# An attention-and-MLP kernel: a 224-byte gap ahead of x's transposed tiles, and the layernorm of tiles 6 and 7 moved behind two evacuations

## The chip, the core and the metric

The kernel runs on one core of a Trainium2 chip. The metric is the device time of one execution in microseconds; the number of record is the median of several runs. A core has five engines that run beside each other, each working through its own instructions in order: TensorE (PE in the profile, with its weight loads shown apart as PEld), VectorE (DVE), ScalarE (ACT), GpSimd (POOL) and SyncE (SP), which here only starts transfers. ScalarE starts some transfers too.

## The reference

Input x has 2048 rows of 512 numbers. The output is x + s * g, with

```python
xn = _layernorm(x)                        # over the 512 columns
q, k, v = xn @ wqkv                       # 32 heads of 16
# each row attends to 8 rows: itself and the rows 2, 4, ..., 14 before it
s = softmax(q . k / 4) @ v, then @ wo
h = relu(xn @ w1 + b1) ** 2               # 1792 wide
g = silu(h @ w2 + b2)
```

All in float32. A product of float32 accuracy is made here of three fast products: each operand is split in a high part and a low part (the rounding error of the high part), and high*high, high*low and low*high are summed (`PASSES`).

## The kernel before

Rows are worked on in 16 tiles of 128 rows. Phase 1 makes, tile by tile, the layernorm, the transpose and the three products q, k and v. Phase 2 runs over 4 chunks of 4 tiles and makes the MLP (`up` writes `ph`, `down` writes `pb`) and the output product (`pw`). VectorE does the sliding attention underneath, in units of 256 rows, from phase 1 on to the end of phase 2; `pump` places its steps in the program by a planner's clock (`clock["PE"]`, `clock["V"]`, priced from constants). Only operations of TensorE and VectorE advance that clock.

Order. Operations of TensorE, VectorE, ScalarE and GpSimd are kept in program order on their engine (`Ordered`). Transfers on SP are ordered by the framework's scheduler; those on ScalarE (the loads of q, k and v for attention) stand in ScalarE's order. Transfers share eight completion semaphores in turn.

Phase 1 in steps, for tile t:

- `load_x(t)` brings x; four buffers `x` in turn.
- `mean(t)` and `spread(t)` (tiles 6 to 15): ScalarE passes over x with a running sum (writing `scratch`), and GpSimd makes `rs` and `shift` of the sums. Tiles 0 to 5 use VectorE's statistics instead (`stats`).
- `norm(t)` writes `xn` (tiles 6 to 15: on ScalarE, from x, `shift` and `rs`) and starts the load of x for tile t + 4. From tile 4 on, two tiles share one buffer `xn`, and there is only one such buffer.
- `shuffle(t)`, t even: four transfers of 128 KB on SP copy `xn` to `xb` with partitions rearranged. The buffer `xn` is free for the next pair when these have landed.
- `trans(t)`: a transpose of `xb` on VectorE into PSUM (`pxT`), then on ScalarE the high part into `xt[t][:, 0]`. `lowx(t)`: VectorE writes the low part. Tiles 0 to 3 are transposed by TensorE and their parts lie in `xT` instead of `xt`.
- `qkv(t, s)`, s = 0, 1, 2 for q, k, v: 12 matrix products `pq` = 128x512, the part of x as weights (stationary), a part of `wq` streamed. Four PSUM buffers in turn. `evacuate(t, s)`: ScalarE copies `pq` to `stg`; after the odd tile of a pair SP stores the pair (`sq`, `sk`, `sv`).

The main loop of phase 1 (`for a in range(2, NT, 2)`, b = a + 1) issues for each pair the six calls `qkv(a,0)`, `qkv(b,0)`, `qkv(a,1)`, `qkv(b,1)`, `qkv(a,2)`, `qkv(b,2)`, and between them the layernorm of the pair a + 4, the transposes of the pair a + 2, and attention steps by `pump`. Ahead of the loop stand `qkv(0,2)`, `norm(4)`, `norm(5)`, `shuffle(4)`, `mean(6)`, `qkv(1,2)`, `spread(6)`, `mean(7)`.

Addresses. Pools of phase 1 are laid out one after the other: `px`, `pstg`, `pxT`. Inside a pool a tile name gets its slots in the order of first use, each slot rounded up to 32 bytes of a partition. From the start of `px` to the first `xt` there are x 4 x 2048 bytes, `st` 2 x 32, `mv` 2 x 32, `rs` 3 x 32, `xb` 2 x 4096, `scratch` 2048, `xn` 4096, `mean` 3 x 32, `shift` 3 x 32 and `stg` 4 x 4096. All weight buffers, the `xT` buffer and the `h` buffers ahead of `px` are multiples of 512 bytes long. Phase 2's pool takes the place of the three pools when they are closed.

Of the kernel before, what the change touches and what calls it, by code (L numbers as in the profile page):

```python
# [8 lines left out]
F32 = mybir.dt.float32  # L9
# [5 lines left out]
P = 128  # L15
# [37 lines left out]
def body(ctx: ExitStack, tc: tile.TileContext, x, wqkv, wo, w1, b1, w2, b2, out):  # L53
# [32 lines left out]
    PE, V, A, G = Ordered(nc.tensor, "PE"), Ordered(nc.vector, "V"), Ordered(nc.scalar), Ordered(nc.gpsimd)  # L86
# [15 lines left out]
    def psA(name):  # L102
        return psum.tile([P, 512], F32, name=name, tag="acc", bufs=4)
# [25 lines left out]

    p1ctx = ExitStack()  # L130
    px, pstg, pxT = (p1ctx.enter_context(tc.tile_pool(name=n, bufs=1)) for n in ("px", "pstg", "pxT"))
    xins = {}


# [4 lines left out]
    def load_x(t):  # L139
        xins[t] = px.tile([P, D], F32, name=f"x{t}", tag="x", bufs=4)  # L140
        dma(xins[t], tile_rows(x, t))
# [217 lines left out]
    def pump(margin=-SLACK):  # L359

        limit = clock["PE"] + margin
        flush(clock["PE"])
        while True:
            if coming[0] is None:
                coming[0] = next(stream, None)
            if coming[0] is None or clock["V"] + coming[0] > limit:
                break
            coming[0] = next(stream, None)
        if coming[0] is None:
            not_before(limit)  # L370
# [4 lines left out]
    def load_w(f):  # L375
        r1, r2 = (piece(f"{n}{f}") for n in ("w1r", "w2r"))
        dma(r1.rearrange("p (k c) -> p k c", c=P), w1[:, f * P:(f + 1) * P].rearrange("(k p) c -> p k c", p=P))
        dma(r2, w2[f * P:(f + 1) * P, :])
        raws[f] = r1, r2

    def next_w():

        f = len(w12)
        if f < NF:
            w12[f] = buffer(f"w{f}", HOME[f]) if f in HOME else p2.tile([P, 2, 2, 512], FR, name=f"w{f}")
            for i, r in enumerate(raws.pop(f)):
                split(w12[f][:, 0, i], w12[f][:, 1, i], r, G)
            if f + 2 < NF:
                load_w(f + 2)


    NT = S // P
# [9 lines left out]
    def small(name, t):  # L402
        return px.tile([P, 1], F32, name=f"{name}{t}", tag=name, bufs=3)

    def scratch(t):
        return px.tile([P, D], F32, name=f"scratch{t}", tag="scratch")
# [6 lines left out]
    def spread(t):  # L413
        rs[t], shifts[t] = small("rs", t), small("shift", t)
        A.activation(scratch(t), xins[t], AF.Square, bias=means[t], accum_out=rs[t])
        G.tensor_scalar(rs[t], rs[t], 1.0 / D, 1e-5, op0=OP.mult, op1=OP.add)
        G.tensor_tensor(rs[t], rs[t], mhalf, op=OP.pow)
        G.tensor_mul(shifts[t], means.pop(t), rs[t])
# [6 lines left out]
    def norm(t):  # L425

        src = xins.pop(t)
        if t < TURN:
            xn[t] = dst = px.tile([P, 2, D], F32, name=f"xn{t}", tag="xb", bufs=2)[:, 0]
        else:  # L430
            if t % 2 == 0:
                xn[t] = px.tile([P, 4, 2, P], F32, name=f"xn{t}", tag="xn")
            dst = xn[t // 2 * 2][:, :, t % 2].rearrange("p a (k c) -> p k a c", k=KT)
            src = src.rearrange("p (k a c) -> p k a c", a=4, k=KT)
        if t < STATS:
            halves = [slice(0, D // 2), slice(D // 2, D)] if t == 0 else [slice(None)]
            for i in halves:
                V.tensor_scalar(dst[:, i], src[:, i], mv[t][:, 0:1], rs[t], op0=OP.subtract, op1=OP.mult)
        else:
            A.activation(dst, src, AF.Identity, bias=shifts.pop(t), scale=rs[t])  # L440
        if t + 4 < NT:
            load_x(t + 4)
# [7 lines left out]
    def shuffle(t):  # L450

        src = xn.pop(t)
        xb[t] = px.tile([P, 4, 2, P], F32, name=f"xb{t}", tag="xb", bufs=2)
        for a in range(4):
            dma(xb[t][32 * a:32 * a + 32].rearrange("p b e c -> p b (e c)"), src[:, a].rearrange("p e c -> p (e c)"))  # L455

    def trans(t):
        place(t)
        pTs[t] = psT(f"pxT{t}")
        if t < TURN:  # L460
            for kt in range(KT):
                PE.transpose(pTs[t][:, kt * P:(kt + 1) * P], xn[t][:, kt * P:(kt + 1) * P], ident)
            seen[t] = clock["PE"] + 800
        else:

            V.transpose(out=pTs[t].rearrange("p (k n b) -> p b k n", k=KT, b=4),
                        in_=xb[t // 2 * 2][:, :, t % 2].rearrange("p b (k c) -> p b k c", k=KT))
            seen[t] = clock["V"] + 800
        A.activation(xt[t][:, 0], pTs[t].rearrange("p (k n) -> p k n", k=KT), AF.Copy)

    def lowx(t):
        not_before(seen.pop(t))
        V.tensor_sub(xt[t][:, 1], pTs.pop(t).rearrange("p (k n) -> p k n", k=KT), xt[t][:, 0].bitcast(F32))
# [3 lines left out]
    def qkv(t, s, between=None, late=False):  # L477

        ps = psA(f"pq{t}_{s}")
        order = [(kt, a, b) for kt in range(KT) for a, b in PASSES]  # L480
        if late:
            order.sort(key=lambda o: o[1])
        for n, (kt, a, b) in enumerate(order):
            PE.matmul(ps, xt[t][:, a, kt], wq[2 * s + kt // 2][:, b, kt % 2, :], start=n == 0, stop=n == 11)
            if between and n == 5:
                between()
        evacuate(t, s, ps)

    def evacuate(t, s, ps):
        if t % 2 == 0:  # L490
            stgs[s] = pstg.tile([P, 4, 2, P], F32, name=f"stg{t}_{s}", tag="stg", bufs=4)
        A.activation(stgs[s][:, :, t % 2], ps.rearrange("p (g c) -> p g c", g=4), AF.Copy,
                     scale=0.25 if s == 0 else 1.0)
        if t % 2:
            r0 = (t - 1) * P + (0 if s == 0 else HALO)
            dst = (sq, sk, sv)[s][:, r0:r0 + UP, :].rearrange("g (p e) c -> p g (e c)", e=2)
            dma(dst, stgs[s].rearrange("p g e c -> p g (e c)"))
            done = done_tiles["qkv"[s]]
            done[0] = t + 1
            done[1][t // 2] = clock["PE"]  # L500
# [8 lines left out]
    def up(c, f):  # L509
        ph = psH(f"ph{c}_{f}")  # L510
        n = 0
        for kt in range(KT):
            for a, b in PASSES:
                PE.matmul(ph.rearrange("p (j n) -> p j n", n=P), w12[f][:, a, 0, kt * P:(kt + 1) * P],
                          xT[c][:, :, b, kt, :], start=n == 0, stop=n == 11)
                n += 1
        if f == NF - 1 and c + 1 < NCH:
            load_xT(c + 1)
        h = hpool.tile([P, 2, 512], FR, name=f"h{c}_{f}", tag="h", bufs=3)
        A.activation(ph, ph, AF.Relu, bias=b1t[:, f:f + 1])  # L520
        A.activation(h[:, 0], ph, AF.Square)
        A.activation(ph, ph, AF.Square)
        hs[f] = h, ph, clock["PE"] + 2000

    def lowh(f):
        h, ph, t = hs[f]
        not_before(t)
        V.tensor_sub(h[:, 1], ph, h[:, 0].bitcast(F32))
# [69 lines left out]
    for a in range(2, NT, 2):  # L598
        b, more, later = a + 1, a + 2 < NT, a + 6 < NT
        if a >= TPC:  # L600
            for t in (a, b):
                dma(sx[t // TPC][:, t % TPC], xt[t].bitcast(F32))
        if a + 4 < NT:
            norm(a + 4)
            spread(b + 4)
        qkv(a, 0)
        pump(LATE)
        if a + 4 < NT:
            norm(b + 4)
            shuffle(a + 4)  # L610
        qkv(b, 0)
        if more:
            trans(a + 2)
        pump(LATE)
        qkv(a, 1)
        if more:
            lowx(a + 2)
            trans(b + 2)
        pump(LATE)
        if not more:  # L620
            up(0, 0)
        qkv(b, 1)
        if more:
            lowx(b + 2)
        if a == 2:
            load_w(0)
            load_w(1)
        else:
            next_w()
        if not more:  # L630
            pump()
            up(0, 1)
            lowh(0)
        pump(LATE)
        qkv(a, 2)
        if later:
            mean(a + 6)
        pump(LATE)
        qkv(b, 2)
        if later:  # L640
            spread(a + 6)
            mean(b + 6)
        if a == NT - 4:
            dma(b1t, b1.rearrange("(f p) -> p f", p=P))
        pump(LATE if more else -SLACK)
# [193 lines left out]
```

## Time and profile before

| what | value |
|---|---|
| median of 3 runs | 502.01 us (501.7 to 502.99) |
| span of the profiled execution, first to last instruction | 500.6 us |
| TensorE (PE) busy | 491.6 us, 98% of the span |
| VectorE (DVE) busy | 422.9 us, 84% |
| ScalarE (ACT) busy | 212.2 us, 42% |
| GpSimd (POOL) busy | 133.4 us, 27% |
| mean granted TensorE clock | 0.997 |

The time of the profiled execution itself is not among those listed; its span lies 1.4 us under the median, and what lies around a span (start and end of the program) is counted in the time alone. In the profile's rows a line such as `38.26 0.81 ACT ... [9.79 <-DMA xb<-xn]` reads: starts at 38.26 us, takes 0.81 us, and the engine sat idle for 9.79 us before it, until the transfer named had landed. Rows of TensorE give the start of a group, the time to the end of its last product, and the count; each product's end is pipelined into the next one's start.

### The profile page before, as it was taken

What the parts mean: (1) busy time and instruction counts of PE and PEld (TensorE: products, weight loads), DVE (VectorE), ACT (ScalarE), POOL (GpSimd) and SP (SyncE); (2) the same over time, 40 slices, a digit from 0 to 9 for tenths busy, and PEclk for the clock granted to TensorE, in tenths of its full rate; (3) what the DMA queues carried; (4) which work ended last, traced back from release to release, by engine and by line L of the source; (5) the groups of instructions that cost most, each with busy time, mean ns of one, the idle gap of its engine ahead of it and who ended that gap; (6) DMA issues with size and microseconds to landing.
All of it is one profiled execution on the core that took longest, in us unless ns stands there. A gap on an engine that the chain in (4) does not pass through costs nothing.

```text
span 500.6 us, 5874 instructions
## 1 busy us (share of the span) xinstructions
PE 491.6 (98%) x2154; PEld 402.8 (80%) x2154; DVE 422.9 (84%) x352; ACT 212.2 (42%) x377; POOL 133.4 (27%) x123
## 2 busy tenths in 40 slices
PE   8997999999999999999999999999999999999997
PEld 6876888888888888888888888888888888888886
DVE  5905599999889699997999998899999889996235
ACT  5526556652344465515424342441254256214331
POOL 1312255343427499200223002041300022220000
PEclk9998999999999999999999999999999999999999
DMA  8996989969966975644216416152333705121022
GB/s 292 283 287 187 324 293 332 289 200 331 310 234 236 206 252 140 201 168 158 101 26 241 156 44 259 67 216 68 117 126 97 269 2 199 43 84 64 22 84 85
DMA packets 48520, 88.79 MB, mean 177 GB/s; under 512 B 5372, under 2 KB 32364, under 8 KB 45676
## 3 DMA queue, kind: packets, MB, share of 16 engines
q1 hardware_dynamic: 44172, 54.87, 35.1%
q10 hardware_dynamic: 4320, 33.56, 18.8%
q8 instruction: 17, 0.28, 0.2%
q14 instruction: 11, 0.09, 0.0%
HBM read 57.94 MB, written 27.32 MB: 170 GB/s over the span
## 4 chain that ended last, share of the span: by engine, by line
PE 95%; DMA 3%; ACT 0%; DVE 0%; SPq 0%; issue 0%; POOL 0%; ACTq 0%; POOLq 0%
PE ph L82 30%; PE pb L82 30%; PE pq L82 25%; PE pw L82 9%; DMA xb<-xn 2%; DMA x<-in_A_x 1%; PE pxT L82 0%; SPq L455 0%; ACT scratch L82 0%; DVE z L82 0%; ACT xn L82 0%; DVE st L82 0%; POOL rs L82 0%; ACT stg L82 0%; DVE xn L82 0%
## 5 line engine op out<-in xcount | busy, mean ns | idle before, releaser
L82 PE MATMUL pb<-w,h 128*128 128x512 f32 x672 | 160.6, 389 | 0.0
L82 PEld LDWEIGHTS pb<-w,h 128*128 128x128 f32 x672 | 126.1, 188 | 26.2
L82 PE MATMUL ph<-xU,w 128*128 128x512 f32 x504 | 120.6, 389 | 0.0
L82 PEld LDWEIGHTS ph<-xU,w 128*128 128x128 f32 x504 | 94.6, 188 | 19.6
L82 ACT ACTIVATE ph<-ph,b1t 128x512 f32<-128x512 f32 x56 | 37.0, 660 | 159.6 <-PE ph L82 150.6
L82 PE MATMUL pq<-wq,xt 128*128 128x512 f32 x432 | 101.3, 395 | 0.0
L82 PEld LDWEIGHTS pq<-wq,xt 128*128 128x128 f32 x432 | 81.1, 188 | 19.7
L82 DVE TENSOR_TENSOR pr<-k,q 128x2048 f32<-128x2048 f32 x32 | 77.6, 2425 | 1.6 <-DMA q<-sq 1.2
L82 DVE TENSOR_TENSOR pv<-v,L 128x2048 f32<-128x2048 f32 x32 | 74.2, 2320 | 0.6
L82 DVE TENSOR_REDUCE L<-pr 128x128 f32<-128x2048 f32 x32 | 72.9, 2278 | 0.6
L82 DVE TENSOR_REDUCE v<-pv 128x256 f32<-128x2048 f32 x32 | 72.9, 2279 | 0.6
L82 DVE TENSOR_TENSOR h<-ph,h 128x512 fp32r<-128x512 f32 x56 | 38.0, 679 | 31.9 <-ACT ph L82 31.9
L82 PE MATMUL pw<-wot,oT 128*128 128x512 f32 (+1 forms) x204 | 45.9, 376 | 0.0
L82 POOL TENSOR_TENSOR z<-z,xr 128x512 f32<-128x512 f32 x12 | 25.5, 2127 | 67.1 <-DVE z L82 57.7
L82 PEld LDWEIGHTS pw<-wot,oT 128*128 128x128 f32 x204 | 36.8, 188 | 7.1
L82 ACT ACTIVATE stg<-pq 128x512 f32<-128x512 f32 x48 | 28.2, 593 | 31.4 <-PE pq L82 28.0
L82 POOL TENSOR_TENSOR w<-w1r,w 128x512 fp32r<-128x512 f32 x14 | 29.4, 2098 | 44.9 <-ACT w L82 40.0
L82 PE MATMUL ph<-xT,w 128*128 128x512 f32 x168 | 40.5, 390 | 0.0
L82 PEld LDWEIGHTS ph<-xT,w 128*128 128x128 f32 x168 | 31.5, 188 | 6.7
L82 PE MATMUL pq<-wq,xT 128*128 128x512 f32 x132 | 32.7, 408 | 3.6 <-ACT stg L82 3.6
L82 ACT ACTIVATE h<-ph 128x512 fp32r<-128x512 f32 x56 | 33.7, 602 | 1.8
L82 PEld LDWEIGHTS pq<-wq,xT 128*128 128x128 f32 x132 | 25.5, 196 | 10.3 <-ACT stg L82 4.1
(64 smaller groups left out, 330.4 us busy)
## 6 DMA issues: line engine op xcount, KB each, us to landing
k<-sk ACTq DMA_DIRECT2D x8, 1408.0 KB, 8.3
v<-sv ACTq DMA_DIRECT2D x8, 1408.0 KB, 6.5
sx<-xt SPq DMA_DIRECT2D x12, 512.0 KB, 6.2
xU<-sx ACTq DMA_DIRECT2D x6, 1024.0 KB, 8.6
x<-in_A_x SPq DMA_DIRECT2D x16, 256.0 KB, 4.5
sk<-stg SPq DMA_DIRECT2D x8, 512.0 KB, 4.5
sq<-stg SPq DMA_DIRECT2D x8, 512.0 KB, 5.8
q<-sq ACTq DMA_DIRECT2D x8, 512.0 KB, 9.0
```

What stands on the lines that cost most here:

```text
L82: return tc.keep_in_program_order(f(*a, **k))
```

## The change

First, a tile of 56 float32 numbers per partition (224 bytes) is made in the pool `pxT` ahead of all others, so the `xt` buffers lie 224 bytes further on; GpSimd clears it once. Second, in the pass a = 2 of the main loop the calls that make the layernorm of tiles 6 and 7 and its rearrangement no longer stand around `qkv(2,0)`, but behind `qkv(3,0)`; the order among them is changed as well.

```diff
     px, pstg, pxT = (p1ctx.enter_context(tc.tile_pool(name=n, bufs=1)) for n in ("px", "pstg", "pxT"))
+    G.memset(pxT.tile([P, 56], F32, name="gap"), 0.0)
     xins = {}
...
         if a >= TPC:
             for t in (a, b):
                 dma(sx[t // TPC][:, t % TPC], xt[t].bitcast(F32))
-        if a + 4 < NT:
+        if 2 < a and a + 4 < NT:
             norm(a + 4)
             spread(b + 4)
         qkv(a, 0)
         pump(LATE)
-        if a + 4 < NT:
+        if 2 < a and a + 4 < NT:
             norm(b + 4)
             shuffle(a + 4)
         qkv(b, 0)
+        if a == 2:
+            spread(7)
+            norm(6)
+            norm(7)
+            shuffle(6)
         if more:
             trans(a + 2)
         pump(LATE)
```

ScalarE's order in that pass was: `norm(6)`, `spread(7)`, evacuation of `qkv(2,0)`, `norm(7)`, evacuation of `qkv(3,0)`, high part of tile 4. It becomes: evacuation of `qkv(2,0)`, evacuation of `qkv(3,0)`, `spread(7)`, `norm(6)`, `norm(7)`, high part of tile 4.

## The prediction

> **What bounds the kernel now.** I read the page first, then TensorE's timeline, then who makes it wait.
>
> ```profile
> span 500.6 us, 5874 instructions
> ...
> PE 95%; DMA 3%; ACT 0%; DVE 0%; SPq 0%; issue 0%; POOL 0%; ACTq 0%; POOLq 0%
> ...
> L82 PE MATMUL pq<-wq,xt 128*128 128x512 f32 x432 | 101.3, 395 | 0.0
> ...
> L82 PE MATMUL pq<-wq,xT 128*128 128x512 f32 x132 | 32.7, 408 | 3.6 <-ACT stg L82 3.6
> ```
>
> The chain that ended last is TensorE for 95% of the span, so time is won only where TensorE idles or runs slower than it can. Two rows are odd: products with weights `xt` take 395 ns, and those with `xT` (tiles 0 to 3) contain an idle time of 3.6 us, ended by an evacuation on ScalarE. TensorE's timeline of the early part:
>
> ```profile
> 20.07 16.60 PE L82 MATMUL pq<-wq,xT 128*128 128x512 f32 x72
> 40.31 7.36 PE L82 MATMUL pq<-wq,xT 128*128 128x512 f32 x24 [3.65 <-ACT stg L82]
> 47.51 22.79 PE L82 MATMUL pq<-wq,xt 128*128 128x512 f32 x97
> ```
>
> and of the change of phases:
>
> ```profile
> 139.91 2.93 PE L82 MATMUL ph<-xT,w 128*128 128x512 f32 x12
> 142.68 2.96 PE L82 MATMUL pq<-wq,xt 128*128 128x512 f32 x12
> 145.48 2.93 PE L82 MATMUL ph<-xT,w 128*128 128x512 f32 x12
> ...
> 156.60 2.88 PE L82 MATMUL pb<-w,h 128*128 128x512 f32 x12
> 159.32 2.88 PE L82 MATMUL ph<-xT,w 128*128 128x512 f32 x12
> ```
>
> From start to start, twelve products take 2.72 us at 156.60 (226.7 ns each), but 2.80 at 142.68. Between 47.51 and 139.91 stand 33 groups, 396 products in 92.40 us: 233.3 ns each. The same by stages (columns: busy us and count of PE, PEld, DVE, ACT, POOL, then granted clock, DMA share, GB/s):
>
> ```profile
> 20.00:36.60 16.60, 16.60 (x75) 13.48 (x73) 4.40 (x11) 4.24 (x10) 2.72 (x7) 1.00 0.94 265
> 36.60:40.30 3.70, 0.07 (x1) 0.00 (x0) 0.73 (x1) 2.00 (x4) 0.36 (x2) 1.00 0.44 147
> ...
> 41.10:44.50 3.40, 3.40 (x9) 2.61 (x8) 1.33 (x2) 2.49 (x5) 0.00 (x0) 0.50 0.44 139
> ...
> 47.50:139.90 92.40, 92.40 (x397) 74.33 (x396) 84.12 (x64) 46.27 (x94) 38.55 (x44) 1.00 0.92 297
> 156.60:210.00 53.40, 53.40 (x237) 44.23 (x236) 47.92 (x33) 29.69 (x52) 38.87 (x22) 1.00 0.77 227
> ```
>
> After the idle time the granted clock is 0.50 for 3.4 us: the stall is paid twice. Why ScalarE is late, and what stands behind it:
>
> ```profile
> 26.43 0.58 ACT L82 ACTIVATE stg<-pq 128x512 f32<-128x512 f32 x1
> ...
> 38.26 0.81 ACT L82 ACTIVATE xn<-x,shift,rs 128x512 f32<-128x512 f32 x1 [9.79 <-DMA xb<-xn]
> 38.98 0.71 ACT L82 ACTIVATE scratch<-x,mean 128x512 f32<-128x512 f32 x1
> ...
> 39.68 0.57 ACT L82 ACTIVATE stg<-pq 128x512 f32<-128x512 f32 x1
> 41.01 0.81 ACT L82 ACTIVATE xn<-x,shift,rs 128x512 f32<-128x512 f32 x1 [0.75 <-POOL shift L82]
> 41.73 0.58 ACT L82 ACTIVATE stg<-pq 128x512 f32<-128x512 f32 x1
> 42.21 0.59 ACT L82 ACTIVATE xt<-pxT 128x512 fp32r<-128x512 f32 x1
> ...
> 44.19 0.60 ACT L82 ACTIVATE xt<-pxT 128x512 fp32r<-128x512 f32 x1 [0.91 <-DVE pxT L82]
> 44.20 0.54 ACTq L82 DMA_DIRECT2D v<-sv  x1
> ...
> 52.69 0.82 ACT L82 ACTIVATE xn<-x,shift,rs 128x512 f32<-128x512 f32 x1 [2.92 <-issue]
> ...
> 54.11 0.58 ACT L82 ACTIVATE stg<-pq 128x512 f32<-128x512 f32 x1
> 56.55 0.81 ACT L82 ACTIVATE xn<-x,shift,rs 128x512 f32<-128x512 f32 x1 [1.86 <-POOL shift L82]
> 57.27 0.58 ACT L82 ACTIVATE stg<-pq 128x512 f32<-128x512 f32 x1
> ```
>
> `norm(6)` (38.26) waits 9.79 us for the one buffer `xn`, until `shuffle(4)` has landed. Behind it stand the evacuations of `qkv(2,0)` (39.68) and `qkv(3,0)` (41.73), whose products (36 and 48 after 20.07) were done at 28.4 and 31.1. TensorE runs on through the four PSUM buffers and stops at `qkv(2,2)`, which needs the first one back.
>
> **The layernorm behind two evacuations.** The two evacuations then run at about 28.5 and 31.2, before ScalarE waits, so `qkv(2,2)` follows at once. The last product before the stall ends at 20.07 + 16.60 = 36.67; a product's end overlaps its successor by 2.88 - 2.72 = 0.16 us, so `qkv(2,2)` can start at 36.51 and `qkv(4,0)` 5.44 us later, at 41.95, instead of 47.51. That is 5.56 us: 3.80 of idle time and 1.76 of half clock.
>
> The wait of `norm(6)` stays; behind it now stand `norm(7)`, the high parts of tiles 4 and 5 and the evacuations of `qkv(2,1)` and `qkv(3,1)`. At ScalarE's own spacing (0.72 us from layernorm to the next instruction, 0.48 per copy) `norm(7)` starts at 38.98, tile 4's high part at 39.70, the evacuation of `qkv(2,1)` at 40.2, tile 5's high part at 41.7, that of `qkv(3,1)` at 42.3. `qkv(4,0)` (41.95) needs the third and `qkv(5,0)` (44.7) the last: they hold by 1.2 and 1.9 us. VectorE's transpose of tile 4 waits for the same landing as before. If that cover were gone, each us would be paid on TensorE.
>
> What is late next is the pair after it.
>
> ```profile
> 35.27 0.39 SPq L497 DMA_DIRECT2D sv<-stg  x1
> 39.10 3.08 SPq L141 DMA_DIRECT2D x<-in_A_x  x2
> 42.27 2.50 SPq L455 DMA_DIRECT2D xb<-xn  x4
> 44.87 0.78 SPq L497 DMA_DIRECT2D sq<-stg  x1
> ```
>
> ```profile
> xb<-xn SPq DMA_DIRECT2D x12, 128.0 KB, 5.4
> ```
>
> ```profile
> 52.64 0.73 DVE L82 STREAM_TRANSPOSE pxT<-xb 128x512 f32<-128x512 f32 x1 [2.60 <-DMA xb<-xn]
> ...
> 58.37 0.69 DVE L82 TENSOR_TENSOR xt<-pxT,xt 128x512 fp32r<-128x512 f32 x1 [2.83 <-ACT xt L82]
> ```
>
> The moved steps issue two loads of x and the four transfers of `shuffle(6)` on SP. These follow `norm(7)`, which starts 2.03 us earlier, so they go out at about 40.24 instead of 42.27. The store `sq` of tiles 2 and 3 (44.87) no longer waits for a late evacuation; I expect it ahead of the loads of x, right behind `sv` at 35.27. Its four pieces go out 0.63 us apart, the last at 42.1. `shuffle(6)` took until 52.6, 8.4 us after its last issue, where a piece lands in 5.4 us at the median (the row of 128 KB): the load of `v` (44.20, on ScalarE) went out with the last piece and I read the rest as time spent behind it. That load follows tile 5's high part and so starts at about 41.7, again ahead of the last piece. I take the landing to move with it, 2.3 us, to 50.3; bounds are 0 (52.6) and 5 (no overtaking: 42.1 + 5.4).
>
> With 2.3 us, the evacuation of `qkv(4,0)` ends at 54.11 + 0.58 - 2.3 = 52.4 and that of `qkv(5,0)`, behind `norm(9)`, at 57.27 + 0.58 - 2.3 = 55.55. TensorE wants these buffers at 36.51 + 6 x 2.72 = 52.83 and 55.55. The second is a tie; for it and for settling I add 0.3 us.
>
> VectorE gains the same 2.3 us and then runs without pause.
>
> ```profile
> 95.35 0.67 DVE L82 TENSOR_TENSOR xt<-pxT,xt 128x512 fp32r<-128x512 f32 x1
> ```
>
> This low part of tile 11 ends at 96.02; the third product of `qkv(11,0)`, 19 groups after 47.51, reads it from 101.2. Of these 5.16 us the new pace takes 5.56 + 19 x 0.08 = 7.08 and VectorE gives 2.3: 0.4 us is left. It just holds. Later the lateness of VectorE (up to 6 us against TensorE) runs into its own idle time:
>
> ```profile
> L82 DVE TENSOR_TENSOR h<-ph,h 128x512 fp32r<-128x512 f32 x56 | 38.0, 679 | 31.9 <-ACT ph L82 31.9
> ```
>
> 31.9 us in phase 2, waiting for what TensorE makes; I count nothing there.
>
> **The gap.** Clearing it is nearest to the other small clears:
>
> ```profile
> 1.24 0.10 POOL L82 MEMSET mhalf<- 128x1 f32 x1
> ```
>
> 0.1 us, beside the wait for the first x. Uncovered it costs 0.1.
>
> Where do the parts lie? From the start of `px` to `xt` the slots sum to 416 bytes modulo 512, and `px` starts where weights start, modulo 512. So `xt` lies 96 bytes short of the weights now; 224 bytes more put it 128 bytes past them. By this count the parts do not lie where the weights do modulo 512; they agree modulo 128 only. The trace shows two cases: difference 0 (`xT`, `h`, all of phase 2), 226.7 ns; difference -96, 233.3 ns. Form, streamed `wq`, clock and traffic are alike (DMA share 0.94 and 0.92), so the address is what is left. 128 bytes is not shown. It may give 226.7, 233.3, or go as far the other way, 240 (or as far below: 220). I take 226.7: 128 is nearer to 0 than to -96 around a period of 512, and equal to 0 for a period of 64 or 128. That wins 432 x 6.67 ns = 2.88 us, and 0.05 us each in the three `ph` groups at 139.91, 145.48 and 153.84, which are disturbed by their neighbours: 3.02 us. If nothing changes it wins nothing; 240 loses 2.88; 220 wins 5.8.
>
> **Sum.** 500.6 - 5.56 - 3.02 + 0.3 = 492.3 us of span. The median, 502.01, stands 1.4 above the span; so 493.7.
>
> **Rivals.**
> - *Address without effect:* the difference of 6.67 ns has another cause than where the part lies, or the 128 bytes are as bad as the 96. For: the count above. Against: no other difference in the rows. 502.0 - 5.56 + 0.1 = 496.5. [...]
> - *A new wait at tile 4:* the landing stays at 52.6. Then `qkv(4,2)` waits from 52.83 to 54.7 and `qkv(5,2)` another 0.4: 2.3 us, and VectorE is late too. 493.4 + 2.3 = 495.7, and 497.5 if the clock halves again for 1.76 us. [...] The one halving here followed 3.65 us, so the trace does not tell.
> - *A worse pace:* 240 ns, 499.3.
> - *Slower:* `shuffle(6)` lands behind the load of `v` and the stores, and TensorE stops at `qkv(4,2)` for longer than the old stall. With L the landing, it starts at L + 2.1, and the loss is L - 50.7 plus 1.76. With the 3.02 us kept it decides from L = 57.5 (loss 8.58), and from 59.0 by over 0.3%. At L = 60, 504.5. For: the tie above. Against: issue is 2 us earlier and the traffic less.
>
> **How the numbers follow.** Forecast 0.50; address without effect 0.20; new wait 0.17; worse pace 0.06; better pace (220, 491) 0.03; slower 0.04. The predicted time is the first. Low 492.6 leaves the better pace out, high 497.5 holds the second and third; left out is 0.13 and some of the edges. A change of 0.3% (1.5 us) is about what a measurement of this kernel can tell from none. Only the last case, and a tail of the worse pace with a new wait, are not faster: faster 0.93, same 0.04, slower 0.03.
>
> **What would show it.** The idle time before `pq<-wq,xT` gone and no stretch of clock 0.50 after 36 us; the wait of `xn` for the transfer still near 38.3; `xt` starting near 42; groups of `pq<-wq,xt` 2.72 us apart; `xn` of tile 8 near 50.4. I am wrong if TensorE idles between 45 and 60 us, if `sq` stands behind `shuffle(6)`, or if groups keep 2.80.

## The result and the profile after

| | before | after |
|---|---|---|
| median of the runs, us | 502.08 (501.7 to 502.99) | 497.98 (496.89 to 498.05) |
| ratio | 1 | 0.9907 [0.9882, 0.9933] |
| span of the profiled execution | 500.6 | 495.8 (time 498.05) |
| first product with `xt` starts at | 47.51 | 41.69 |
| 396 products from there to the first `ph` group | 92.40 | 93.45 |

4.1 us are won, where 8.3 were forecast (493.7). The time lies 0.5 us above the upper end of the forecast range (497.5). On another chip the same kernel gave 497.33 against 502.17, the same ratio.

The page of the changed kernel (span, the chain of waits, one group of products):

```profile
span 495.8 us, 5876 instructions
...
PE 92%; DMA 4%; issue 1%; ACT 1%; SPq 1%; POOL 1%; DVE 0%; ACTq 0%; POOLq 0%
...
L82 PE MATMUL pq<-wq,xt 128*128 128x512 f32 x432 | 101.5, 395 | 0.9 <-ACT stg L82 0.8
```

Two things are read here at once. The products with weights `xt` still take 395 ns each, as before: no new pace. And the group now contains an idle time of 0.9 us that it did not have, ended by an evacuation on ScalarE. TensorE's timeline, early and at the change of phases:

```profile
19.80 22.06 PE L82 MATMUL pq<-wq,xT 128*128 128x512 f32 x96
41.69 11.32 PE L82 MATMUL pq<-wq,xt 128*128 128x512 f32 x48
53.81 71.50 PE L82 MATMUL pq<-wq,xt 128*128 128x512 f32 x305 [0.79 <-ACT stg L82]
...
135.14 2.94 PE L82 MATMUL ph<-xT,w 128*128 128x512 f32 x12
137.91 2.96 PE L82 MATMUL pq<-wq,xt 128*128 128x512 f32 x12
140.71 2.92 PE L82 MATMUL ph<-xT,w 128*128 128x512 f32 x12
...
154.51 2.88 PE L82 MATMUL ph<-xT,w 128*128 128x512 f32 x12
```

The 96 products with `xT` run through without a pause: the stall is gone. At 53.81, at `qkv(4,2)`, a smaller one has come. The group at 137.91 still takes 2.80 us to the next one. By stages (same columns as in the prediction):

```profile
36.60:47.50 10.90, 10.90 (x49) 8.91 (x48) 6.62 (x6) 6.78 (x14) 1.86 (x3) 1.00 0.94 273
47.50:139.90 92.40, 91.54 (x393) 73.62 (x392) 84.39 (x64) 46.24 (x93) 38.54 (x42) 1.00 0.91 299
```

The granted clock is 1.00 from 36.60 to 139.90; before, it read 0.50 from 41.10 to 44.50. ScalarE, SP's queue and VectorE around the moved steps:

```profile
28.29 0.60 ACT L82 ACTIVATE stg<-pq 128x512 f32<-128x512 f32 x1
31.01 0.60 ACT L82 ACTIVATE stg<-pq 128x512 f32<-128x512 f32 x1 [2.12 <-PE pq L82]
38.87 1.52 ACT L82 ACTIVATE xn<-x,shift,rs 128x512 f32<-128x512 f32 x2 [6.57 <-DMA xb<-xn]
...
42.27 0.53 ACTq L82 DMA_DIRECT2D v<-sv  x1
...
51.75 0.82 ACT L82 ACTIVATE xn<-x,shift,rs 128x512 f32<-128x512 f32 x1 [4.29 <-DMA xb<-xn]
...
53.18 0.57 ACT L82 ACTIVATE stg<-pq 128x512 f32<-128x512 f32 x1
```

```profile
34.96 0.39 SPq L498 DMA_DIRECT2D sv<-stg  x1
35.44 0.49 SPq L498 DMA_DIRECT2D sq<-stg  x1
...
40.86 2.50 SPq L456 DMA_DIRECT2D xb<-xn  x4
```

```profile
51.69 0.73 DVE L82 STREAM_TRANSPOSE pxT<-xb 128x512 f32<-128x512 f32 x1 [3.58 <-DMA xb<-xn]
```

The two evacuations stand at 28.29 and 31.01, ahead of the wait of `xn` for `shuffle(4)`, which is still there (38.87). `shuffle(6)` lands at 51.7. `norm(8)` waits for it, and behind `norm(8)` stands the evacuation of `qkv(4,0)` (53.18 to 53.75), for which `qkv(4,2)` waits at 53.81.

### The profile page after: what moved, and what is told of

It is laid out like the page before. It is cut to its first block, busy times and chain, and to the rows that moved or that the text cites. A ratio compares the mean times of both kernels' runs of the same rounds, so it can differ in the third digit from the quotient of the medians.

```text
span 495.8 us, 5876 instructions
## 1 busy us (share of the span) xinstructions
PE 489.3 (99%) x2154; PEld 401.6 (81%) x2154; DVE 424.0 (86%) x352; ACT 211.8 (43%) x377; POOL 132.9 (27%) x124
## 4 chain that ended last, share of the span: by engine, by line
PE 92%; DMA 4%; issue 1%; ACT 1%; SPq 1%; POOL 1%; DVE 0%; ACTq 0%; POOLq 0%
PE ph L82 31%; PE pb L82 31%; PE pq L82 21%; PE pw L82 9%; DMA xb<-xn 3%; SPq L456 1%; DMA x<-in_A_x 1%; POOL rs L82 0%; ACT xn L82 0%; PE pxT L82 0%; ACT scratch L82 0%; DVE z L82 0%; DVE st L82 0%; ACT stg L82 0%; DVE xn L82 0%
## 5 line engine op out<-in xcount | busy, mean ns | idle before, releaser
L82 DVE TENSOR_TENSOR pv<-v,L 128x2048 f32<-128x2048 f32 x32 | 75.4, 2356 | 0.6
L82 POOL TENSOR_TENSOR L<-L,mx_None 128x512 f32<-128x512 f32 x7 | 15.5, 2217 | 68.0 <-DVE mx_None L82 68.0
L82 ACT ACTIVATE ph<-ph 128x512 f32<-128x512 f32 x56 | 33.3, 595 | 0.0
```

What stands on the lines that cost most here:

```text
L82: return tc.keep_in_program_order(f(*a, **k))
```

## The experiments

Twelve runs, eight of them in the table. "Difference" is the address of the loaded part of x (`xt`, the stationary operand) less that of the streamed `wq`, modulo 512 bytes. By the program's allocation `wq` lies at 480, `xt` at 384 before and at 96 with the gap of 56 floats: differences -96 and 128, as the prediction counted them. A gap of 24 floats puts `xt` at 480 too: difference 0.

| version | difference | layernorm moved | median, us | ratio to before |
|---|---|---|---|---|
| e1_move_only | -96 | yes | 496.99 | 0.9897 [0.9872, 0.9923] |
| e2_gap56_only | 128 | no | 502.39 | 0.9995 [0.9973, 1.0017] |
| e3_gap24_move | 0 | yes | 495.23 | 0.9861 [0.9832, 0.9891] |
| e4_gap24_only | 0 | no | 499.83 | 0.9948 [0.9927, 0.9969] |
| f1_after_again | 128 | yes | 497.33 | 0.9907 [0.9884, 0.993] |
| f2_v_later | 128 | yes, load of `v` later | 496.83 | 0.9893 [0.9872, 0.9914] |
| f3_gap24_v_later | 0 | yes, load of `v` later | 494.32 | 0.9849 [0.9824, 0.9874] |
| f4_gap24_all_behind | 0 | in every pass | 494.30 | 0.9849 [0.9823, 0.9874] |

The e runs share one chip (before: 501.97), the f runs another (502.17). The g runs are single executions on a third chip (before: 501.33) and are read by their pace: g1 took 495.50 us, g2 496.16, g3 497.44, g4 499.22.

**The move alone (e1).** The changed kernel without the gap:

```diff
-    G.memset(pxT.tile([P, 56], F32, name="gap"), 0.0)
```

> The layernorm moved, no gap (xt 96 bytes short of the weights, as before the change). Theory A (pace is set by where x's parts lie against the weights modulo 512 bytes; only difference 0 gives 226.7 ns): pace 233.3 ns, the 3.65 us stall gone, short stalls of about 1 us and 0.3 us left at qkv(4,2) and qkv(5,2); time within 0.5 us of the changed kernel, 497.5 to 498.5. Theory B (the address has no effect on the pace): the same. If the gap of 224 bytes is worth what I forecast, this is 3 us slower than the changed kernel (501).

The first `xt` product starts at 41.75; the first `ph` group follows at 134.15, 92.40 us later, as before. TensorE's timeline, and ScalarE's:

```profile
134.15 2.93 PE L82 MATMUL ph<-xT,w 128*128 128x512 f32 x12
136.91 2.96 PE L82 MATMUL pq<-wq,xt 128*128 128x512 f32 x12
```

```profile
40.08 0.52 ACTq L82 DMA_DIRECT2D v<-sv  x1
...
48.98 0.82 ACT L82 ACTIVATE xn<-x,shift,rs 128x512 f32<-128x512 f32 x1 [3.71 <-DMA xb<-xn]
```

So the move carries the whole gain of the change. The wait at `qkv(4,2)` is absent here, although the program is the same but for the gap: in this execution `shuffle(4)` landed 2.2 us earlier (`norm(6)` at 36.67, not 38.87), so the load of `v` went out earlier and `shuffle(6)` landed earlier (tile 6 is transposed at 48.91, not 51.69).

**The gap alone (e2).** Before, with the gap line of 56 floats added:

> The gap of 224 bytes alone, layernorm as before. Theory A: difference +128 is not 0, pace 232 to 233 ns, time 501.5 to 502.2 (no change against before to be told). Theory B: the same. The forecast's 226.7 ns would give 499.1.

```profile
39.13 8.59 PE L82 MATMUL pq<-wq,xT 128*128 128x512 f32 x24 [2.79 <-ACT stg L82]
47.56 82.66 PE L82 MATMUL pq<-wq,xt 128*128 128x512 f32 x355
```

```profile
139.59 2.89 PE L82 MATMUL ph<-xT,w 128*128 128x512 f32 x12
142.32 2.96 PE L82 MATMUL pq<-wq,xt 128*128 128x512 f32 x12
```

From 47.56 to 139.59 are 92.03 us for the 396 products: 232.4 ns each, 0.9 less than before. The median shows no difference.

**Difference 0, with and without the move (e3, e4).** One number is changed:

```diff
-    G.memset(pxT.tile([P, 56], F32, name="gap"), 0.0)
+    G.memset(pxT.tile([P, 24], F32, name="gap"), 0.0)
```

> The layernorm moved, and a gap of 24 numbers (96 bytes) instead of 56: x's parts lie where the weights do modulo 512. Theory A: pace of pq<-wq,xt 226.7 ns, 2.5 to 2.9 us off phase 1, of which the waits at qkv(4,2) and qkv(5,2) take back 0.4: about 495.5. Theory B: pace stays 232 to 233, 498.0.

> The gap of 24 numbers alone, layernorm as before, so nothing but the pace can change and there are 3.7 us or more of slack at every evacuation. Theory A: 226.7 ns, 502.1 - 3.0 = 499.1. Theory B: 502.1.

TensorE in e4, the stall still in it:

```profile
38.88 7.15 PE L82 MATMUL pq<-wq,xT 128*128 128x512 f32 x24 [2.54 <-ACT stg L82]
45.87 84.48 PE L82 MATMUL pq<-wq,xt 128*128 128x512 f32 x372
...
135.63 2.88 PE L82 MATMUL ph<-xT,w 128*128 128x512 f32 x12
138.35 2.88 PE L82 MATMUL pq<-wq,xt 128*128 128x512 f32 x12
141.07 2.88 PE L82 MATMUL ph<-xT,w 128*128 128x512 f32 x12
...
154.67 2.88 PE L82 MATMUL ph<-xT,w 128*128 128x512 f32 x12
```

45.87 to 135.63 are 89.76 us: 226.67 ns a product. The group at 138.35 takes 2.72 us; the disturbance that `ph` groups had beside `xt` groups (2.77 us at 139.91 before, 2.72 at 135.63 here) is gone as well. The median of e4 falls by 2.14 us, and the interval of its ratio holds 3.0. So the address is the cause of the slow pace, and the prediction's 3.02 us are there, at another gap than the change sets. In e3 the row of these products between 44 and 130 us reads 389 ns with 0.1 us of idle time:

```profile
L82 PE MATMUL pq<-wq,xt 128*128 128x512 f32 x379 | 86.4, 389 | 0.1
```

Its `xt` stage takes 41.73 to 131.91, 90.18 us: 0.42 more than 89.76. Tiles 4 and 5, where a wait was expected, run without one. The time is lost at `qkv(11,2)`, near 104.6, which needs the buffer of `qkv(11,0)` back, and that evacuation stands behind `norm(15)`, which waits for GpSimd:

```profile
103.23 0.82 ACT L82 ACTIVATE xn<-x,shift,rs 128x512 f32<-128x512 f32 x1 [2.64 <-POOL shift L82]
103.95 0.58 ACT L82 ACTIVATE stg<-pq 128x512 f32<-128x512 f32 x1
```

**The same kernel on another chip (f1).**

> The changed kernel once more, on the same chip as the next three. Theory A: the 224-byte gap is worth 0.3 us at most, so 497.0 to 498.2, and about 1.3 us of waits at qkv(4,2) and qkv(5,2) when the landing of shuffle(6) is as late as 51.6.

In its profiled execution, 499.03, the six products `pq<-wqraw,scratch` from 6.98 took 4.74 us (2.84 from 6.66 in the changed kernel's), `xt` began 2.2 us later, at 43.90, and the evacuations were in time; the other five executions lie between 496.8 and 497.6. From `xt`'s start to the first `ph` group it took 92.03 us, as e2 did without a wait.

**What holds `shuffle(6)` up (f2).** The changed kernel, where only the deferred load of `v` is given a later due time:

```diff
-  defer(max(clock["V"] + FREE if u else 0, done_tiles[n][1][u] + LAND), start)
+  defer(max(clock["V"] + FREE if u else 0, done_tiles[n][1][u] + LAND
+            + (8000 if (n, u) == ("v", 0) else 0)), start)
```

> The changed kernel with the first load of v started later (on ScalarE just ahead of norm(8) instead of behind the high part of tile 5). Theory V (that load overtakes shuffle(6) and sets its landing): shuffle(6) lands at 46 to 48 instead of 51.6, xn of tile 8 starts near 48 (then GpSimd's shift ends last), the waits at qkv(4,2) and qkv(5,2) vanish, 496.5. Rival (the stores beside it set the landing): it stays at 50 to 52 and the time at 498.

```profile
42.34 0.61 ACT L82 ACTIVATE stg<-pq 128x512 f32<-128x512 f32 x1
44.83 0.52 ACTq L82 DMA_DIRECT2D v<-sv  x1
45.96 0.81 ACT L82 ACTIVATE xn<-x,shift,rs 128x512 f32<-128x512 f32 x1 [0.47 <-POOL shift L82]
```

```profile
46.04 0.72 DVE L82 STREAM_TRANSPOSE pxT<-xb 128x512 f32<-128x512 f32 x1
```

The pieces of `shuffle(6)` went out from 38.87 to 41.37. Tile 6 is transposed at 46.04 with no wait for a transfer, and `norm(8)` waits for GpSimd only. From issue to landing a piece took 4.1 us at the median, against 8.8 in the changed kernel (1.4 MB of `v` beside it) and 8.3 in e1. With the load of `v` beside them tile 6 was transposed 8.4 to 9.4 us after that load was issued, in every run: 44.20 and 52.64 before, 42.27 and 51.69 after, 40.08 and 48.91 in e1, 40.39 and 49.68 in e3. The load of `v` is what holds them up; the stores, the rival named, went out right behind the pieces as before. 41.61 to 133.64 are 92.03 us: with this difference of 128, that is the stage without any wait, and the 93.45 of the changed kernel hold 1.42 us of waiting.

**Both corrections (f3), and another order (f4).** f3 is f2 with the gap of 24 floats. f4 leaves the load of `v` and puts the layernorm of every pass behind both evacuations:

```diff
         qkv(a, 0)
         pump(LATE)
+        qkv(b, 0)
+        if a + 4 < NT:
+            spread(b + 4)
+            norm(a + 4)
             norm(b + 4)
             shuffle(a + 4)
-        qkv(b, 0)
```

> The same with a gap of 24 numbers, so that x's parts lie where the weights do modulo 512. Theories A and V together: pace 226.7 ns and no waits of TensorE on ScalarE in phase 1: 494.0. If VectorE is the bound by then (0.8 us of slack at tile 11 with the aligned gap and the landing at 49.6), nothing is gained over 495.2.

> Gap of 24 numbers, and in every pass of the loop (not in a = 2 alone) the layernorm of the pair a + 4 stands behind the two evacuations. If the waits at qkv(4,2) and qkv(5,2) come from evacuations standing behind norm(8), they vanish whatever the landing is, and tile 6's high part comes earlier too: 494.2 to 494.8. Rival: the layernorm is now too late for shuffle, and TensorE waits at qkv(8,0) or later: above 495.5.

In f4, ScalarE's rows and TensorE's group between 44 and 130 us:

```profile
41.59 0.52 ACTq L82 DMA_DIRECT2D v<-sv  x1
...
50.85 1.52 ACT L82 ACTIVATE xn<-x,shift,rs 128x512 f32<-128x512 f32 x2 [2.05 <-issue]
```

```profile
L82 PE MATMUL pq<-wq,xt 128*128 128x512 f32 x381 | 86.5, 389 | 0.0
```

`norm(8)` still runs only at 50.85, but the evacuations of `qkv(4,0)` and `qkv(5,0)` stand ahead of it, and TensorE does not wait: 41.86 to 131.62, 89.76 us. f3 and f4 agree (span 491.9 in both) and are the fastest versions run, 3 us below the changed kernel on the same chip (f1). From f2 to f3, where only the difference goes from 128 to 0, the median falls by 2.51 us; the traces give 2.27 (92.03 to 89.76) and 0.28 at the change of phases. Two ways lead to the same end: land the transfer earlier, or let nothing wait behind it.

**Which differences are good (g1, g2, g3).** In each, the tiles of pass a = 4, 8, 12 lie at one difference and those of 6, 10, 14 at another: in g1 and g2 by two pairs of buffers with a gap ahead of each, in g3 by slices that start 4 floats or 1 float into a larger tile. The gap lines of g1 (g2: 32 and 104):

```diff
+    G.memset(pxT.tile([P, 88], F32, name="gap"), 0.0)
...
+    if t == 6:
+        G.memset(pxT.tile([P, 80], F32, name="gap2"), 0.0)
+    xt[t] = pxT.tile([P, 2, KT, P], FR, name=f"xt{t}", tag=f"xt{t // 2 % 2}", bufs=2)
```

> The layernorm moved, and the four xt buffers laid out by hand: tiles 4, 5, 8, 9, 12, 13 lie 256 bytes past the weights modulo 512, tiles 6, 7, 10, 11, 14, 15 lie 64 bytes past. Theory A (only difference 0 modulo 512): both keep 231 to 238 ns. A period of 256: the first six run at 226.7 ns. Periods of 64 or 128 are excluded already by the 224-byte gap (difference 128, 232.4 ns).

> The same with differences of 32 bytes (tiles 4, 5, 8, 9, 12, 13) and -64 bytes (6, 7, 10, 11, 14, 15). Theory A: both at 230 to 238 ns. If a difference within some 64 bytes of 0 is good enough, both at 226.7.

> The same with differences of 16 bytes (tiles 4, 5, 8, 9, 12, 13) and 4 bytes (the others). Theory A taken strictly: neither is at 226.7. If what counts is a line of 16 or 32 bytes, the tiles at 4 bytes are at 226.7.

The same group cut by the first five passes (389 ns goes with 226.7 from start to start, 395 with 233.3: a product's end overlaps its successor by 162 ns). g1, differences 256, 64, 256, 64, 256 (the row of the fifth pass reads as that of the third):

```profile
L82 PE MATMUL pq<-wq,xt 128*128 128x512 f32 x73 | 16.7, 389 | 0.0
L82 PE MATMUL pq<-wq,xt 128*128 128x512 f32 x61 | 14.4, 396 | 0.0
L82 PE MATMUL pq<-wq,xt 128*128 128x512 f32 x64 | 14.7, 389 | 0.0
L82 PE MATMUL pq<-wq,xt 128*128 128x512 f32 x59 | 13.9, 396 | 0.0
```

g2, the first two passes, differences 32 and -64:

```profile
L82 PE MATMUL pq<-wq,xt 128*128 128x512 f32 x70 | 16.5, 395 | 0.0
L82 PE MATMUL pq<-wq,xt 128*128 128x512 f32 x62 | 14.4, 391 | 0.0
```

g3, differences 16, 4, 16, 4, 16. The first pass is cut in two, ahead of and behind a wait of 0.79 us at `qkv(4,2)`; the fourth pass reads nearly as the second (14.1, 394) and is left out:

```profile
L82 PE MATMUL pq<-wq,xt 128*128 128x512 f32 x48 | 11.0, 389 | 0.0
L82 PE MATMUL pq<-wq,xt 128*128 128x512 f32 x11 | 2.7, 395 | 0.0
L82 PE MATMUL pq<-wq,xt 128*128 128x512 f32 x62 | 14.6, 394 | 0.0
L82 PE MATMUL pq<-wq,xt 128*128 128x512 f32 x64 | 14.7, 389 | 0.0
L82 PE MATMUL pq<-wq,xt 128*128 128x512 f32 x62 | 14.6, 396 | 0.0
```

From start to start the means are 227.0 ns at 256, 233.3 at 64, 233.3 at 32, 229.0 at -64, 232.4 at 4. At 16 two paces occur: 226.7 in the third pass, 233.3 in the fifth. In the first pass the 48 products ahead of the wait run at 226.7, and the next products of tile 4, behind it, at some 233.5. Of the nine differences run (with -96, 0 and 128), only 0 and 256 hold the fast pace wherever they stand; in g1's third and fifth pass the first twelve products take 229.1 and 229.2 on average, all that follow 226.7. 16 can hold either, so the difference is not all. The change of pace across the wait suggests that the moment at which a group begins counts too; no run here tests that, and none tells why.

**Is it the place or the difference? (g4)** The changed kernel without the gap, and a pad of 24 floats in the first pool, ahead of the weights, so that `xt` lies at 480 (the good place of e3 and e4) and the streamed weights at 64: difference -96 again.

```diff
+    G.memset(const.tile([P, 24], F32, name="pad"), 0.0)
...
-    G.memset(pxT.tile([P, 56], F32, name="gap"), 0.0)
```

> The layernorm moved, no gap, but every buffer (weights and x's parts alike) lies 96 bytes further: xt at 480 modulo 512, where it is fast with the gap of 24, the weights at 64; the difference is -96 as before the change. If the difference counts: pq<-wq,xt 233.3 ns, phase 2 226.7. If xt's own place counts: pq<-wq,xt 226.7. If the weights' own place counts: phase 2 changes.

Its `xt` products began only at 43.78 (41.75 in e1), a late start as in f1, so its time (499.22) is not compared. Its pace is that of before: 43.78 to 136.18 are 92.40 us, 233.3 ns a product, and phase 2, in which both operands lie elsewhere too, keeps its 389 ns a product. It is the difference that counts, not the place of either operand.

## Why the prediction was right in one half and wrong in the other

It was made of four terms, three on the span (500.6 to 492.3) and one from span to time; the span became 495.8. Of its three signs of being wrong two came: TensorE idles at 53.81, and groups keep 2.80.

- *The stall, 5.56: right.* `xt` starts 5.82 earlier, of which 0.27 come from the start (20.07 to 19.80): 5.55. The mechanism is the one told: the evacuations stand ahead of the wait, the wait stays, the half clock is gone. `sq` went out right behind `sv`, as expected. By the medians the move is worth 4.98 (e1): the half clock, 1.76 of the 5.56, was read from one execution and does not come in each (last section).
- *The pace, 3.02: wrong.* The stage without waits takes 92.03 instead of 92.40, and from the first `ph` group to the one behind the first `pb` group pass 19.37 (135.14 to 154.51) instead of 19.41 (139.91 to 159.32): 0.41 in all. The failing step is the choice "226.7: 128 is nearer to 0 than to -96 around a period of 512, and equal to 0 for a period of 64 or 128". 64 and 128 are no periods (233.3 ns in g1, 232.4 in e2). 0 and 256 agree (226.7 in e4, 227.0 in g1), so if there is a period it is 256, and 128 is half of one. The count of the addresses was right, and so was the reading that the address is the cause (e4: 89.76 instead of 92.40 in the stage and 19.04, 135.63 to 154.67, instead of 19.41 at the change of phases: 3.01 of 3.02). With 56 floats the parts do not lie where the weights do modulo 512, as it had counted; with 24 they do. The prediction counted 128 and gave the case in which nothing changes too small a chance beside the one that it took.
- *What is late next, 0.3: right place, too small.* The waits cost 1.42 in the profiled execution (f2's stage against the changed kernel's); by the medians on the other chip, f1 and f2, they cost 0.5, so their size scatters. The landing was to move by 2.3, from 52.6 to 50.3; it moved by 0.95, to 51.7, because `shuffle(4)` landed 0.6 later than before and the load of `v` therefore went out at 42.27, not 41.7, and because the landing then came 9.4 us after that load instead of 8.4. The tie was forecast at `qkv(5,2)`; it broke one group earlier. That it is a tie, e1 and f2 show, in which TensorE did not wait. In both `shuffle(6)` landed earlier, in e1 because `shuffle(4)` did: its landing fell between 36.7 and 38.9 in the runs here. VectorE's cover of 0.4 us at tile 11 held: at the full new pace f3 and f4 run the stage in 89.76 without a wait.
- *From span to time, 1.4: 2.25 here* (498.05 - 495.8). A later execution of the kernel before shows the same (502.67 and 500.4), so the 1.4, a median less another execution's span, was too little.

These close: 2.61 of pace, 1.12 of waits, 0.27 gained at the start and 0.85 around the span make 493.7 + 4.3 = 498.0, against 498.05.

Of the rivals, *address without effect* has nearly the right sum for a kernel without the new wait (496.5; f2 measured 496.83 on its chip). It named two reasons. That something else than the address sets the pace is refuted by e4: 233.3 ns became 226.7 when only the address of the loaded weights changed. That 128 bytes are as bad as 96 is nearly what happened (232.4 and 233.3). *A new wait at tile 4* happened, smaller, and without the half clock that it was to bring in its dearer case; with the landing at 51.7, `qkv(4,2)` began 2.1 us later, as counted there.

## What to carry to other kernels

Where two groups of products of one form show two durations, as 395 and 389 ns here, compare the addresses of their loaded and streamed operands, and aim for the very difference that the fast group has; a difference that is merely closer has no claim to its pace (4 bytes gave 232.4 ns from start to start, 0 gave 226.7). An evacuation that TensorE needs soon is not queued behind an instruction that waits for a transfer or for another engine (as at `qkv(11,2)` in e3): an order that lets nothing wait behind the transfer (f4) was worth as much here as landing it earlier (494.30 us in f4, 494.32 in f3), and leaves more room for a transfer that lands late in a given run. Before a stall is counted as gone, look up which transfer bounds the next pass, and how far its landing scatters.

## What the runs showed of the hardware that was not expected

- The pace of the 128x512 products went with the difference of the addresses of the loaded and the streamed operand, modulo 512 bytes: 226.7 ns at 0 (e4, f4) and, but for the first twelve products of two passes, at 256 (g1); 229.0 at -64 (g2), 232.4 at 4 (g3) and 128 (e2), 233.3 at -96 (before, g4), 32 (g2) and 64 (g1); at 16 either (g3). Over 432 products the 6.67 ns between 226.7 and 233.3 are 2.9 us.
- The granted clock read 0.50 after an idle time of TensorE of 3.65 us in the kernel before, but also beside one of 2.54 us in e4 and one of 2.79 in e2, where the half clock lasted twice as long. The rows of e4 and of e2:

```profile
38.90:41.10 2.20, 2.20 (x5) 1.80 (x6) 0.00 (x0) 1.52 (x3) 0.57 (x2) 0.50 0.33 108
```

```profile
40.00:46.80 6.80, 6.80 (x20) 5.31 (x20) 4.46 (x5) 4.49 (x9) 0.65 (x1) 0.61 0.80 217
```

  In the kernel before the clock reads 0.50 for 3.4 us, from 41.12 to 44.54. In e4 its mean is 0.92 over 36.20:38.90 and 0.88 over 41.10:44.50, in e2 0.89 over 36.20:39.10 and 0.50 over 39.10:40.00; worked out from these means and the rows above, an estimate, the half clock lasted some 3.4 us in e4 and 6.8 in e2 and began near 38.5 in both, in e4 some 2.1 us into the idle time, which ran from 36.34 to 38.88. Before, it began 0.81 us after the idle time had ended, at 40.31. Beside the 0.79 us of idle time ahead of 53.81 in the changed kernel the clock stayed at 1.00. What decides when it falls and for how long, no run here shows.
- So one stall costs differently from run to run. The 23 executions of the kernel before on one chip spread from 499.58 to 504.04; the granted clock of the two fastest (499.58 and 500.21) reads 1.000, that of the three slowest (from 503.51) 0.992 to 0.993. For comparison, the profiled execution of e2, with its 6.8 us at half clock, reads 0.992, and that of the kernel before, with 3.4 us, 0.997. e1, in which TensorE does not stall, spreads from 496.85 to 497.17.
- A load of 1.4 MB issued on ScalarE's queue held up pieces of 128 KB issued on SP's in the same microseconds by some 5 us, and unevenly: in the changed kernel the four pieces took 4.0 to 9.1 us from issue to landing, 8.8 at the median, against 4.1 in f2, where the load went out at 44.83, behind the pieces.
